# Two decode layers on one core: one batch's first block of K kept in a PSUM bank between the layers, and one bank for all small and idle products

## The chip, the cores and the metric

The kernel runs on one core of a Trainium2 chip, in one launch. The metric is the device time of a launch in microseconds (us). Every engine of the core (TensorE or PE, VectorE or DVE, ScalarE or ACT, GpSimd or POOL, SyncE or SP) has its own queue of instructions; the queues meet through semaphores, which the tile framework sets from the regions that instructions read and write.

## The reference

A decode step for 4 batch rows of width 512: an attention block and a gated feed-forward, and then both again with the same weights and the same K and V caches. All values are fp32. Cut to what matters:

```python
B, D, Hq, Hkv, Sk, Dh, F = 4, 512, 32, 8, 4096, 128, 1792
def A(x):                                    # attention against the cache
    q = heads(x @ wq)                        # 32 heads; 4 of them share one of 8 K/V groups
    p = softmax(q . k_cache * Dh ** -0.5)    # 4096 keys
    return concat(p @ v_cache) @ wo
def Bf(x):                                   # gated feed-forward
    return (silu(x @ w1) * (x @ w3)) @ w2
x = x + A(layernorm(x)); x = x + Bf(layernorm(x))
x = x + A(layernorm(x)); x = x + Bf(layernorm(x))
```

K and V hold 4 x 8 x 4096 x 128 values each, 64 MB a cache and 128 MB for both, and each layer needs all of them. On chip there is room for some 27 MB, so almost everything is read twice.

## The kernel before, in words

**Storage.** One SBUF tile, `arena`, holds everything that is loaded: 216 units of 256 fp32 columns (`KB`), 128 KB of data to a unit over the 128 partitions. `take` and `give` hand out units when the program is built, `load` appends an entry to a list `plan`, and `pump` issues the next entries of that list on SyncE's DMA queue (L183) as soon as their units are free in the list's bookkeeping; on the chip each issue then waits until the engines have done with what lay there. So the order of loads is fixed by hand, and each load goes out when its place falls free. `loaded` names the units of a key, `done` and `vacate` free them.

**Attention.** The groups of K/V heads are worked in turn, 0 to 7 in the first layer and 7 to 0 in the second, so that group 7 (`TURN`) ends one layer and begins the next; its V, and `wq` and `wo`, stay in the arena. `scores` multiplies the padded queries `qpad` with K in 8 blocks (`NB`) of 512 keys (`BK`); in each block it has one matmul for each batch row `b` (L393), all into the bank `s_ps`. `factors` and `exponents` make the softmax's numerators, `turn_p` transposes them, `weigh` multiplies them with V into `o_ps` (L438), and `project_o` adds `oT` times `wo` to `x_ps`, either by `whole` (two matmuls of 512 columns, L473) or by `pair` (four of 256, L466).

**The turn between the layers.** In the first layer's feed-forward (`feed_forward`, `keep` true) w1, w3 and w2 pass through 7 slots of 4 units that are used round and round. Behind the last piece of w2 the same slots take K of group 7 for its first 4 blocks (`SPLIT`) in pieces called `half`: 8 pieces, 2 to a block, each for 2 of the 4 batch rows. Piece 7 and what follows go where `wq` lies, and so wait for the second layer's Q products (`q_product`, L337). `collect` closes a residual sum: it copies `x_ps` to the SBUF tile `p` (L314, L316), turns it by matmuls into a small product in PSUM (L320, L323), adds that to `xc` (L324), and returns `mean`, a further small product (L329) that VectorE subtracts from `mu` (L330). `project_q` then makes the queries: it copies the first group's Q product to `p`, turns it (`q_turn`, L348) into `qpad` (L374), and yields the products of the other groups as steps that stand between other work on PE.

**Small and idle products.** `misc` hands out a small PSUM area, from the two banks `m_ps0` and `m_ps1` in turn. `busy(n)` puts matmuls on PE whose result nobody reads (L281), up to three units of 128 columns in each, into the bank that `misc` did not hand out last. The sum of squares of a layer norm is such a small product too (`total`, L290, read at L300).

PSUM has eight banks: `s_ps`, `o_ps`, `t_ps`, `x_ps`, `m_ps0`, `m_ps1`, and `kept0` and `kept1`, in which `stash` keeps the first piece of `wo` over the turn.

Of the kernel before, what the change touches and what calls it, by code (L numbers as in the profile page):

```python
# [8 lines left out]
F32 = mybir.dt.float32  # L9
# [7 lines left out]
P = 128  # L17
KC = D // P
NB = 8
BK = SK // NB  # L20
# [12 lines left out]
TURN = HKV - 1  # L33
# [5 lines left out]
def tile_decode_layers(ctx: ExitStack, tc: tile.TileContext, x, kt, v, wq, wo, w1, w3, w2, w2s, out):  # L39
    nc = tc.nc  # L40
# [3 lines left out]
    psum = ctx.enter_context(tc.tile_pool(name="psum", bufs=1, space=bass.MemoryType.PSUM))  # L44
# [72 lines left out]
    def piece(name, i, at):  # L117

        w, layer, lo, n, per = {"w1a": (w1, 0, 4 * i, 4, 4), "w3a": (w3, 0, 4 * i, 4, 4),
                                "w1b": (w1, 0, 16 + 3 * i, 3, 3), "w3b": (w3, 0, 16 + 3 * i, 3, 3),  # L120
                                "w2": (w2, 0, 4 * i, 4, 2), "half": (kt[TURN], 1, 4 * i, 4, 4)}[name]
        weights(name, w[:, lo * KB:(lo + n) * KB], layer, (n,), per, at, 2 * i if name == "w2" else i)

    RING = KEPT + 64
# [67 lines left out]
    def loaded(*key):  # L192
        a, n, _ = where[key]
        return arena[:, a * KB:(a + n) * KB]
# [60 lines left out]
    o_ps = psum.tile([P, 512], F32, name="o_ps")  # L255
    t_ps = psum.tile([P, 4, P], F32, name="t_ps")
    x_ps = psum.tile([P, 512], F32, name="x_ps")
    m_ps = [psum.tile([P, 512], F32, name=f"m_ps{i}") for i in range(2)]
    kept = [psum.tile([P, 512], F32, name=f"kept{i}") for i in range(2)]
    nc.vector.memset(x_ps, 0.0)  # L260

# [6 lines left out]
    turn = {"m": 0}  # L268

    def misc(n=B):  # L270
        turn["m"] ^= 1
        return m_ps[turn["m"]][:, 0:KC * n].rearrange("p (k c) -> p k c", k=KC)

    def flat(a):
        return a.rearrange("p k b -> p (k b)")
# [1 line left out]
    def busy(n=1):  # L277

        while n > 0:
            w = min(n, 3)  # L280
            nc.tensor.matmul(m_ps[turn["m"] ^ 1][0:32, (4 - w) * P:], rows, ident.unsqueeze(1).broadcast_to([P, w, P]),  # L281
                             start=True, stop=True)
            n -= w

# [66 lines left out]
    def project_q(layer, steps, mean):  # L351
        one_ps = t_ps.rearrange("p i r -> p (i r)")
        sq = squares()
        q_product(layer, steps[0], one_ps, 0, True, True)
        m = total(flat(sq))
        q_copy(one_ps)
        rstd = deviation(sq, m)
        nc.vector.tensor_scalar(scaled, rows, rstd, SCALE, op0=ALU.mult, op1=ALU.mult)
        rest = list(enumerate(steps[1:]))

        def products():
            for j, g in rest:
                q_product(layer, g, o_ps, j, j == 0, j == HKV - 2)
                yield
            q_copy(o_ps)
            yield
            nc.vector.tensor_copy(qT, q_turn(32))
            yield
        more = products()
        if layer:  # L370
            next(more)
            next(more)
        m = q_turn(B)
        nc.vector.tensor_copy(qpad[:, :, PAD:PAD + REP], m.rearrange("p h b -> p b h"))  # L374
        if layer:
            next(more)
        mean()
        return more
# [5 lines left out]
    def scores(layer, g, pieces=iter(())):  # L384
        for blk in range(NB):
            split = layer == 1 and g == TURN and blk < SPLIT
            keys = [("half", layer, 2 * blk + i) for i in range(2)] if split else [("k", layer, g, blk)]
            lo = PAD - REP * blk
            for i, key in enumerate(keys):
                k = loaded(*key).rearrange("p (b s) -> p b s", s=BK)  # L390
                for j in range(B // len(keys)):
                    b = i * B // len(keys) + j
                    nc.tensor.matmul(s_ps[32 * b:32 * b + 32, :], qpad[:, b, lo:lo + 32], k[:, j, :],  # L393
                                     start=(blk == 0), stop=(blk == NB - 1))
            for key in keys:
                done(*key)
            next(pieces, None)
# [32 lines left out]
    def weigh(layer, g, st, pieces=iter(()), fill=False):  # L430
        for f in range(2):
            for i in range(NI):
                if fill and f and i == NI // 2:
                    busy(9)
                key = ("v", 0 if g == TURN else layer, g, NI * f + i)
                w = loaded(*key).rearrange("p (b n) -> p b n", b=B)
                for b in range(B):
                    nc.tensor.matmul(o_ps[32 * b:32 * b + 32, :], pT[:, i, 32 * b:32 * b + 32], w[:, b, :],  # L438
                                     start=(i == 0), stop=(i == NI - 1))
                if g != TURN or layer:  # L440
                    done(*key)
                yield
            next(pieces, None)
            if f == 0:
                nc.scalar.activation(p, o_ps, AF.Copy, scale=st["parts"][:, 0:1])  # L445
            else:
                nc.vector.scalar_tensor_tensor(p, o_ps, st["parts"][:, 1:2], p, op0=ALU.mult, op1=ALU.add)  # L447
        if fill:
            busy(2)
        for j in range(4):  # L450
            nc.tensor.transpose(t_ps[:, j, :], p[:, j * P:(j + 1) * P], ident)  # L451
        if fill:
            busy()

        own = t_ps[:, :, :]
        own = bass.AP(own.tensor, own.offset, [own.ap[0], (1, REP), (32, B), (P + 4, 4), (16, 2)])
        raw = small("raw", REP * B)
        nc.vector.tensor_reduce(raw.rearrange("p (h b) -> p h b", b=B), own, axis=AX.XY, op=ALU.add)
        nc.vector.tensor_tensor(oT[:, g].rearrange("p h b -> p (h b)"), raw, st["r"], op=ALU.mult)  # L459
# [24 lines left out]
    def project_o(layer, g, first=False, last=False):  # L484
        for i in range(2):
            n = 2 * g + i
            key = ("wo", 0, n)
            w = loaded(*key).rearrange("p (h e) -> p h e", e=D)
            if last or not layer and g == TURN - 1:
                pair(i, lambda h: oT[:, g, h, :], lambda j: w[:, j, :], False, last and i == 1)  # L490
            else:
                whole(i, lambda h: oT[:, g, h, :], lambda j: w[:, j, :], first)
            if layer or n == 0:
                vacate(*key)
            if not layer and i == (g < TURN):
                busy({3: 6, 5: 3, 6: 2, 7: 2}.get(g, 0))

    def feed_forward(layer, mean):
        keep = layer < LAYERS - 1
# [48 lines left out]
        if not keep:  # L548
            for k in range(KC):
                nc.tensor.matmul(x_ps[32 * k:32 * k + B, 0:P], xt[:, k, :], ident, start=True, stop=False)  # L550
            busy(5)
        gate(0, FA)
        join(0, FA)
        product("w1b", s_ps, FA, FB, (1, 1, 1, 1))
# [48 lines left out]
    for layer in range(LAYERS):  # L603
# [28 lines left out]
        if layer == 0:  # L632
            give(PT, ARENA - PT)
            pump()
            stash()

            busy(15)
            for g in range(HKV):
                project_o(layer, g, g == 0, g == TURN)
        else:  # L640
            project_o(layer, before[0], False, True)
# [46 lines left out]
```

## Time and profile before

| | before |
|---|---|
| time, median of 3 runs | 705.85 us (705.85 to 705.91) |
| the profiled execution | 705.91 us |
| its span, first to last instruction | 704.1 us |
| read from HBM | 298.85 MB, 425 GB/s over the span |
| PE, VectorE, ScalarE busy | 408.4, 85.1, 36.8 us (58, 12 and 5%) |
| mean granted clock of PE | 0.81 of full speed |

How to read it: busy shares are means over stages. The share of busy DMA engines and the GB/s in a window say whether the stream of loads runs without a gap. The chain of waits is followed back from the last instruction and says what the end hung on. In a row of the timeline the first number is the start, the second the duration, and what stands in brackets is how long the engine was idle before it and what released it. An fp32 matmul is two passes over PE, so it counts twice in "x".

### The profile page before, as it was taken

How to read it: one execution, taken by the hardware profiler on the slowest of the kernel's cores; microseconds unless marked ns; L12 is line 12 of the kernel's file. 1: busy time of each engine (PE TensorE's matmuls, PEld its weight loads, DVE VectorE, ACT ScalarE, POOL GpSimd, SP SyncE). 2: the span in 40 equal slices, each digit the busy share in tenths (PEclk: the TensorE clock that was granted, in tenths of full speed). 3: DMA queues.
4: the chain of work that ended last, by engine and by line, in shares of the span. 5: the costliest groups of instructions: out<-in, count | busy, mean ns of one | idle time of the engine just before them, and what ended most of it. 6: DMA issues, size and time to landing. Idle time of an engine off the chain costs nothing. (4 is left out here: it accounts for less than half of the span.)

```text
span 704.1 us, 7082 instructions
## 1 busy us (share of the span) xinstructions
PE 408.4 (58%) x3174; PEld 136.0 (19%) x3174; DVE 85.1 (12%) x291; ACT 36.8 (5%) x85; POOL 2.9 (0%) x10
## 2 busy tenths in 40 slices
PE   2555453456556454547788894364553545477687
PEld 1112011112111111112243231021120111122134
DVE  2001010101001010101111111011000101010111
ACT  0000000000000000002001000000000000000100
POOL 0000000000000000000000000000000000000000
PEclk9986787767777776879999988679787868689899
DMA  9999999999999999999999999999999999999997
GB/s 417 432 403 473 418 417 422 462 418 432 451 421 422 436 448 421 440 408 435 410 405 403 410 437 440 439 436 422 432 455 417 433 432 440 421 433 420 426 425 298
DMA packets 13749, 299.37 MB, mean 425 GB/s; under 512 B 1671, under 2 KB 1799, under 8 KB 6407
## 3 DMA queue, kind: packets, MB, share of 16 engines
q1 hardware_dynamic: 13584, 298.92, 99.2%
q8 instruction: 25, 0.41, 0.2%
q14 instruction: 5, 0.04, 0.0%
q10 hardware_dynamic: 135, 0.01, 0.0%
HBM read 298.85 MB, written 0.07 MB: 425 GB/s over the span
## 5 line engine op out<-in xcount | busy, mean ns | idle before, releaser
L438 PE MATMUL o_ps<-arena 128*32 128x512 f32 x1024 | 148.6, 730 | 147.8 <-DMA arena<-in_v 133.0
L393 PE MATMUL s_ps<-arena,qpad 128*32 128x512 f32 x1024 | 146.2, 725 | 88.0 <-DMA arena<-in_kt 88.0
L438 PEld LDWEIGHTS o_ps<-arena 128*32 128x32 f32 x1024 | 37.7, 130 | 256.8 <-issue 224.5
L393 PEld LDWEIGHTS s_ps<-arena,qpad 128*32 128x32 f32 x1024 | 39.3, 130 | 178.1 <-issue 170.6
L447 DVE SCALAR_TENSOR_TENSOR p<-o_ps,parts,p 128x512 f32<-128x512 f32 x16 | 12.0, 751 | 272.7 <-PE o_ps L438 272.7
L400 DVE TENSOR_REDUCE top<-s_ps 128x1 f32<-128x512 f32 x16 | 11.1, 691 | 190.8 <-PE s_ps L393 190.8
L281 PE MATMUL m_ps<-ident,rows 128*32 128x256 f32 (+2 forms) x90 | 25.2, 376 | 0.0
L445 ACT ACTIVATE p<-o_ps,parts 128x512 f32<-128x512 f32 x16 | 11.0, 687 | 195.8 <-PE o_ps L438 186.9
L337 PE MATMUL o_ps<-arena,xpad 128*32 128x512 f32 x112 | 15.4, 675 | 7.8 <-DMA arena<-in_wq 7.8
L424 PE MATMUL t_ps<-ident,p 128*128 128x128 f32 x64 | 11.4, 305 | 13.5 <-ACT p L418 13.5
L451 PE MATMUL t_ps<-ident,p 128*128 128x128 f32 x64 | 10.5, 287 | 13.9 <-DVE p L447 13.8
L411 ACT ACTIVATE f<-d 128x1 f32<-128x1 f32 x16 | 3.2, 203 | 253.1 <-DVE d L409 253.1
L473 PE MATMUL x_ps<-arena,oT 128*4 128x512 f32 x104 | 12.8, 592 | 6.3 <-DVE oT L459 3.5
L418 ACT ACTIVATE p<-s_ps,top 128x512 f32<-128x512 f32 x16 | 10.9, 684 | 76.7 <-PE t_ps L451 76.7
L425 DVE COPY arena<-t_ps 128x512 f32<-128x512 f32 x16 | 11.1, 691 | 9.7 <-PE t_ps L424 9.7
L451 PEld LDWEIGHTS t_ps<-ident,p 128*128 128x128 f32 x64 | 6.7, 141 | 28.0 <-DVE p L447 28.0
L424 PEld LDWEIGHTS t_ps<-ident,p 128*128 128x128 f32 x64 | 7.3, 150 | 22.3 <-ACT p L418 19.2
L281 PEld LDWEIGHTS m_ps<-ident,rows 128*32 128x32 f32 x90 | 9.4, 110 | 10.4 <-issue 6.3
L506 PE MATMUL o_ps<-arena,xpad 128*32 128x192 f32 (+1 forms) x128 | 8.1, 360 | 1.3 <-DMA arena<-in_w 1.2
L506 PE MATMUL s_ps<-arena,xpad 128*32 128x192 f32 (+1 forms) x128 | 7.9, 359 | 1.6 <-DMA arena<-in_w 1.5
L337 PEld LDWEIGHTS o_ps<-arena,xpad 128*32 128x32 f32 x112 | 3.6, 122 | 17.2 <-DMA arena<-in_wq 8.7
L533 PE MATMUL x_ps<-arena,qT 128*4 128x128 f32 (+1 forms) x168 | 5.9, 271 | 1.1 <-DMA arena<-in_w 1.1
(100 smaller groups left out, 137.3 us busy)
## 6 DMA issues: line engine op xcount, KB each, us to landing
arena<-in_v SPq DMA_DIRECT2D x4, 4096.0 KB, 37.3
arena<-in_w SPq DMA_DIRECT2D x17, 512.0 KB, 9.3
arena<-in_kt SPq DMA_DIRECT2D x8, 1024.0 KB, 10.5
arena<-in_kt SPq DMA_DIRECT2D x2, 4096.0 KB, 16.9
arena<-in_wq SPq DMA_DIRECT2D x1, 7168.0 KB
arena<-in_v SPq DMA_DIRECT2D x3, 2048.0 KB, 36.9
arena<-in_wo SPq DMA_DIRECT2D x1, 4096.0 KB, 24.5
arena<-in_kt SPq DMA_DIRECT2D x8, 512.0 KB, 8.0
```

The costliest lines, as they stand in the source:

```text
L281: nc.tensor.matmul(m_ps[turn["m"] ^ 1][0:32, (4 - w) * P:], rows, ident.unsqueeze(1).broadcast_to([P, w, P]), start=True, stop=True)
L337: nc.tensor.matmul(ps[32 * k:32 * k + 32, :], xpad[:, k, lo:lo + 32], w[:, k, :], start=first, stop=last)
L393: nc.tensor.matmul(s_ps[32 * b:32 * b + 32, :], qpad[:, b, lo:lo + 32], k[:, j, :], start=(blk == 0), stop=(blk == NB - 1))
L400: nc.vector.tensor_reduce(top[:, 0:1], s_ps, axis=AX.X, op=ALU.max, negate=True)
L424: nc.tensor.transpose(t_ps[:, i, :], p[:, i * P:(i + 1) * P], ident)
L425: nc.vector.tensor_copy(pT.rearrange("p i r -> p (i r)"), t_ps.rearrange("p i r -> p (i r)"))
L438: nc.tensor.matmul(o_ps[32 * b:32 * b + 32, :], pT[:, i, 32 * b:32 * b + 32], w[:, b, :], start=(i == 0), stop=(i == NI - 1))
L445: nc.scalar.activation(p, o_ps, AF.Copy, scale=st["parts"][:, 0:1])
L447: nc.vector.scalar_tensor_tensor(p, o_ps, st["parts"][:, 1:2], p, op0=ALU.mult, op1=ALU.add)
L451: nc.tensor.transpose(t_ps[:, j, :], p[:, j * P:(j + 1) * P], ident)
L473: nc.tensor.matmul(x_ps[r:r + B, :], left(2 * i + n), w(n), start=first, stop=False)
L506: nc.tensor.matmul(ps[32 * j:32 * j + 32, lo:lo + n], x32[:, k, :], w[:, j * n:(j + 1) * n], start=(k == 0), stop=(k == KC - 1))
```

## The change

In the first layer, once PE has issued the matmuls of group 7's block 0, ScalarE copies batch row 0's 512 columns of that block to a PSUM bank of their own, `keptk`. In the second layer, after the turned query has been copied out, ScalarE copies them back to `p`, and the score matmul of row 0 and block 0 reads `p`. Piece 0 of `half` is then 2 units (row 1 alone) in place of 4, so 256 KB less are loaded. The bank comes from `m_ps`: `misc` hands out columns 0 to 127 and 128 to 255 of one bank in turn, and `busy` writes columns 256 to 511 of the same bank, at most two units a matmul. Some counts of `busy` are smaller, and group 6's projection in the first layer goes by `whole`.

```diff
-                                "w2": (w2, 0, 4 * i, 4, 2), "half": (kt[TURN], 1, 4 * i, 4, 4)}[name]
+                                "w2": (w2, 0, 4 * i, 4, 2), "half": (kt[TURN], 1, 4 * i if i else 2, 4 if i else 2, 4 if i else 2)}[name]
...
-    m_ps = [psum.tile([P, 512], F32, name=f"m_ps{i}") for i in range(2)]
+    m_ps = psum.tile([P, 512], F32, name="m_ps")
+    keptk = psum.tile([P, BK], F32, name="keptk")
...
         turn["m"] ^= 1
-        return m_ps[turn["m"]][:, 0:KC * n].rearrange("p (k c) -> p k c", k=KC)
+        lo = P * turn["m"]
+        return m_ps[:, lo:lo + KC * n].rearrange("p (k c) -> p k c", k=KC)
...
-            w = min(n, 3)
-            nc.tensor.matmul(m_ps[turn["m"] ^ 1][0:32, (4 - w) * P:], rows, ident.unsqueeze(1).broadcast_to([P, w, P]),
+            w = min(n, 2)
+            nc.tensor.matmul(m_ps[0:32, (4 - w) * P:], rows, ident.unsqueeze(1).broadcast_to([P, w, P]),
...
         if layer:
+            nc.scalar.copy(p, keptk)
             next(more)
...
-                    nc.tensor.matmul(s_ps[32 * b:32 * b + 32, :], qpad[:, b, lo:lo + 32], k[:, j, :],
+                    if split and b < 2 and blk == 0:
+                        this = k[:, 0, :] if b else p
+                    else:
+                        this = k[:, j, :]
+                    nc.tensor.matmul(s_ps[32 * b:32 * b + 32, :], qpad[:, b, lo:lo + 32], this,
...
+            if g == TURN and blk == 0 and not layer:
+                nc.scalar.copy(keptk, loaded(*keys[0])[:, 0:BK])
...
@@ weigh
-                    busy(9)
+                    busy(6)
...
@@ project_o
-            if last or not layer and g == TURN - 1:
+            if last:
...
-                busy({3: 6, 5: 3, 6: 2, 7: 2}.get(g, 0))
+                busy({3: 6, 5: 2, 6: 2, 7: 2}.get(g, 0))
...
@@ feed_forward
-            busy(5)
+            busy(4)
...
@@ tile_decode_layers
-            busy(15)
+            busy(14)
```

## The prediction, made before the changed kernel was run

> **What bounds the kernel now.** I read the head of the page first, then the end of the chain of waits, then windows and the timeline around the turn between the layers, and last the timeline of the tail.
>
> ```profile
> DMA  9999999999999999999999999999999999999997
> HBM read 298.85 MB, written 0.07 MB: 425 GB/s over the span
> ```
> All 40 slices but the last show the 16 DMA engines nine tenths busy or more: the span is the time of 298.85 MB.
>
> ```profile
> 685.54 15.05 DMA arena<-in_w
> 700.63 0.45 PE x_ps L533 x8
> ```
> This is how the chain of waits ends: the last weights are issued at 685.54 and land 15.05 us later behind everything queued before them; from 700.63 PE, VectorE and the output's transfer take the remaining 3.5 us of the span of 704.1. The end is therefore set by bytes, unless the queue runs empty somewhere or PE falls behind the stream in the tail.
>
> ```profile
> 363.00:373.00 10.00, 8.10 (x101) 3.61 (x93) 1.18 (x4) 1.91 (x3) 0.00 (x0) 1.00 1.03 404
> 375.00:388.00 13.00, 11.30 (x106) 4.58 (x104) 2.44 (x12) 0.85 (x3) 0.55 (x1) 1.00 1.02 401
> ...
> 386.00:388.00 2.00, 2.00 (x19) 0.54 (x19) 0.89 (x5) 0.37 (x1) 0.55 (x1) 1.00 1.03 412
> 388.00:390.00 2.00, 2.00 (x21) 1.14 (x17) 0.17 (x1) 0.00 (x0) 0.00 (x0) 1.00 1.07 385
> 390.00:392.00 2.00, 2.00 (x22) 0.82 (x22) 0.16 (x1) 0.00 (x0) 0.00 (x0) 1.00 0.97 379
> 392.00:394.00 2.00, 2.00 (x24) 0.65 (x20) 0.00 (x0) 0.00 (x0) 0.00 (x0) 1.00 1.02 401
> ```
> These windows end in granted clock, DMA share and GB/s. The first holds mostly pieces of 384 KB (3 KB a partition), the second pieces of 512 KB (4 KB a partition): 404 against 401 GB/s, so row length hardly matters there. The four slices are the place to watch: at 388 to 392 the rate falls to 385 and 379 between 412 and 401. Against 412 that is 27 and 33 GB/s for 2 us each, 0.12 MB or 0.3 us. Here the queue is lean.
>
> **The change, part by part.**
>
> *Fewer bytes.* Piece 0 of the half shrinks from 512 to 256 KB: batch 0 of block 0 is no longer read again. At the stage's 401 GB/s, 262,144 bytes are 0.65 us; at the span's 425 they are 0.62; at the slowest slice of the turn, 379, they are 0.69. What remains has rows of 2 KB, which no run shows by themselves. At worst such a row takes as long as one of 4 KB, and the saving is 0; the nearest rows, 3 KB at 404, say that time follows bytes. I take 0.65.
>
> *The copy into the kept bank (layer 0).*
>
> ```profile
> 299.44 4.48 PE L393 MATMUL s_ps<-arena,qpad 128*32 128x512 f32 x40
> 300.55 3.76 SPq L183 DMA_DIRECT2D arena<-in_v  x4
> 305.73 0.20 ACT L411 ACTIVATE f<-d 128x1 f32<-128x1 f32 x1 [16.59 <-DVE d L409]
> ```
> ```profile
> L418 ACT ACTIVATE p<-s_ps,top 128x512 f32<-128x512 f32 x16 | 10.9, 684 | 76.7 <-PE t_ps L451 76.7
> ```
> The added ScalarE copy of 128x512 costs about 0.68 us (the L418 group). It waits for group 7's K, as PE does at 299.44, so it runs to about 300.2. ACT has been idle for 16.59 us before 305.73, so nothing is queued behind it. The buffer's next user is the DMA of 300.55, later than the copy's end. Cost 0; without that cover the load would be issued up to 0.7 us later, and with nothing else queued the stream would be late by as much.
>
> *The copy back (layer 1).*
>
> ```profile
> 388.00 1.05 PE L348 MATMUL m_ps<-scaled,p 128*128 128x4 f32 x8
> 389.09 0.17 DVE L374 COPY qpad<-m_ps 128x16 f32<-128x16 f32 x1 [1.41 <-PE m_ps L348]
> 389.98 0.38 PE L329 MATMUL m_ps<-off,both 128*128 128x4 f32 x2
> 390.29 1.06 PE L393 MATMUL s_ps<-arena,qpad 128*32 128x512 f32 x8
> 402.13 1.06 PE L393 MATMUL s_ps<-arena,qpad 128*32 128x512 f32 x8 [1.05 <-DMA arena<-in_kt]
> ```
> ACT may overwrite `p` when PE has read it, at 389.05, and ends near 389.8; the first score matmul comes at 390.29. There is 0.5 us of cover from the third Q product. Without it PE would lose at most the 0.7, and it waits 1.05 us for K at 402.13 anyway. ACT has no other work before the second half of Q is copied, after all Q products. Cost 0. SP and GpSimd are passed by neither copy, and the number of DMAs stays.
>
> *One bank for small products and idle products.* Column ranges stay apart, but the bank is now shared, so a write of PE must wait until VectorE has read the last small product.
>
> ```profile
> 383.19 0.38 ACT L316 ACTIVATE p<-x_ps 128x256 f32<-128x256 f32 x1 [11.44 <-DVE p L314]
> 384.18 0.37 PE L323 MATMUL m_ps<-off,both 128*128 128x16 f32 x2
> 384.49 0.41 PE L281 MATMUL m_ps<-ident,rows 128*32 128x128 f32 x2
> 384.60 0.17 DVE L324 TENSOR_TENSOR xpad<-xpad,m_ps 128x16 f32<-128x16 f32 x1 [0.74 <-PE m_ps L323]
> 384.82 1.06 PE L337 MATMUL t_ps<-arena,xpad 128*32 128x512 f32 x8
> ```
> That disjoint halves of one bank are kept apart is seen already: ScalarE takes columns 256 to 511 of `x_ps` only when VectorE has done with columns 0 to 255 (its row at 383.19 was released by VectorE's L314, which reads those). [...] By address alone the next two costs would be 0 and the sum unchanged, since both are covered.
>
> First, the idle product that ends `collect`. It now runs under VectorE's add (384.49 beside 384.60). With one bank it starts only after that read, at 384.8, exactly when the next real product could, and pushes it by its own length: 0.21 us if passes follow each other (9 units take 2.10 us below, with 0.2 of fill), 0.41 if not. Three places; I take 0.21 each.
>
> ```profile
> 684.74 0.36 PE L329 MATMUL m_ps<-off,both 128*128 128x4 f32 x2
> 684.93 0.17 DVE L300 SCALAR_TENSOR_TENSOR sq<-m_ps,pick 128x16 f32<-128x16 f32 x1 [2.14 <-PE m_ps L290]
> 685.10 1.93 PE L506 MATMUL o_ps<-arena,xpad 128*32 128x256 f32 x32
> ...
> 688.88 1.51 PE L506 MATMUL s_ps<-arena,xpad 128*32 128x192 f32 x32 [0.57 <-DMA arena<-in_w]
> 697.45 1.06 PE L533 MATMUL x_ps<-arena,qT 128*4 128x128 f32 x32 [0.45 <-DMA arena<-in_w]
> ```
> Second, `mean` in each feed-forward: L329 follows the sum of squares, which VectorE reads at 684.93 to 685.10. It slides from 684.74 to about 685.1, and the products behind it, with VectorE's update of the mean, by 0.36. Elsewhere the reader is long done before PE returns to the bank (389.26 against 389.98).
>
> Do these delays reach the end? In the tail PE waits 0.57 and 0.45 us for weights. It is late by 0.21 + 0.36, and `busy(5)` to `busy(4)` gives back 0.21: net 0.36, which is less than the 0.57 at 688.88. Everything before that starts from V's landing and moves up with the stream. Cost 0; were that wait under 0.36, the rest would pass into the end.
>
> *Fewer idle products, and `whole` for `pair`.*
>
> ```profile
> 672.62 2.10 PE L281 MATMUL m_ps<-ident,rows 128*32 128x384 f32 x6
> 675.29 1.92 PE L438 MATMUL o_ps<-arena 128*32 128x512 f32 x16 [0.58 <-DMA arena<-in_v]
> ...
> 352.39 1.05 PE L466 MATMUL x_ps<-arena,oT 128*4 128x256 f32 x16
> 424.05 1.04 PE L473 MATMUL x_ps<-arena,oT 128*4 128x512 f32 x8
> ```
> `busy(9)` to `busy(6)` takes 3 x 0.21 us from a stretch after which PE waits 0.58 for V: 0, and it lets PE take V up to 0.65 earlier. Group 6's projection by `pair` takes 1.05 us in 16 matmuls, `whole` 1.04 in 8: 0.
>
> *The lean queue at the turn.*
>
> ```profile
> 382.72 0.33 SPq L183 DMA_DIRECT2D arena<-in_kt  x1
> 385.92 0.33 SPq L183 DMA_DIRECT2D arena<-in_kt  x1
> ```
> ```profile
> arena<-in_kt SPq DMA_DIRECT2D x8, 512.0 KB, 8.0
> out<-p SPq DMA_DIRECT2D x1, 64.0 KB, 1.6
> ```
> After 382.72 the next load waits for the first Q product and is issued 3.2 us later. A 512 KB piece lands 8.0 us after its issue, of which about 1.6 is latency (what the lone output transfer takes) and 1.3 its own move: some 5.1 us are queued ahead as a rule. Pieces come 1.3 us apart while the stream is even, so the gap uses up 1.9 and leaves 3.2, or 1.6 beyond the latency, as an estimate and a mean over 16 engines. The change takes 0.65 of queued work and adds 0.21 of delay: 0.7 us left. Since the rate dips already, some engines run dry sooner. The loss lies between 0 (the last engine never runs dry) and 0.86 (it has no margin now). I take 0: 0.7 stays positive, and what counts at the end is the engine that finishes last.
>
> **Sum.** -0.65 + 0 = -0.65. The profiled execution took 705.91, the median is 705.85: 705.26 against the first, 705.20 against the second. I predict 705.2, 0.09% faster. About 0.2%, 1.41 us, is what a measurement of this kernel can tell from no change.
>
> **Rivals.**
> *Nothing gained* (0.18): the turn eats it, or rows of 2 KB move at half the rate: 705.85; with the whole 0.86 lost, 706.06. For it: 385 and 379 GB/s at 388 to 392. Against: the 0.7 us left.
> *More than the bytes* (0.10): the dip of 0.3 us closes too, as the copy leaves less to fetch before the turn: 704.9. Against: Q's product, not the piece, sets the issue at 385.92.
> *Slower, by the clock* (0.06).
>
> ```profile
> 404.00:406.00 2.00, 0.12 (x1) 0.13 (x2) 1.18 (x6) 0.87 (x3) 0.00 (x0) 0.62 1.03 430
> ```
> ```profile
> 338.81 3.41 PE L281 MATMUL m_ps<-ident,rows 128*32 128x384 f32 x10
> 344.98 3.62 PE L473 MATMUL x_ps<-arena,oT 128*4 128x512 f32 x32 [2.75 <-DMA arena<-in_wo]
> ```
> PE idles 2.75 us before 344.98, and `busy(14)` makes that 2.96. If the granted clock halves there, as it does at 404 (0.62 in the first row) after a gap of 2.7 (403.19, the end of the score matmuls that began at 402.13, to 405.88), the 3.62 us of projection become 7.2 and the loads that wait for them go out up to 3.6 late. With no cover from the queue that gives 708.8. It decides for "slower" when over 2.06 of it (the 0.65 gained and 1.41) passes the cover; against it stands a cover of some 5 us as long as pieces follow each other evenly. [...]
>
> **Chances and range.** The forecast has 0.64, and 0.02 is left for what no row shows. Faster by over 1.41 us has 0.05: 0.04 of the 0.10, should more than the dip close, and half of the 0.02, since no row has 1.41 us to give. Slower by over that has 0.07: the clock case and the other half. The rest lies within 1.41 us: 0.88. The range runs from the closed dip, with 0.1 beyond it, to the turn that loses all 0.86, with 0.1 beyond it: 704.8 to 706.2.
>
> **What the profile after would show.** HBM read 298.59 MB; an ACT copy of 0.7 us at 299.5 and one near 389; the last idle product of `collect` behind VectorE's add, and L329 behind L300; the last weights landing 0.65 earlier; at 388 to 392 a rate not under 375. Wrong would be: a slice at the turn far below that, PE no longer waiting for weights at 688 and 697, or a clock under 1.00 between 340 and 400.

## The result, and the profile after

| | before | after |
|---|---|---|
| time, median of 13 runs each, run beside each other | 706.01 us (705.85 to 706.93) | 707.82 us (706.34 to 708.88) |
| ratio, with its 95% interval | | 1.002 (1.0013 to 1.0028) |
| the profiled execution, its span | 705.91, 704.1 us | 707.88, 706.1 us |

By the medians the changed kernel is 1.8 us slower (0.9 to 2.0 by the interval), where 0.65 us less were forecast. Fewer bytes were read, as told, and the rate fell by more. The page of the changed kernel:

```profile
HBM read 298.59 MB, written 0.07 MB: 423 GB/s over the span
```
298.59 MB is the figure of the prediction. Three long windows tell where the rate was lost. Each row ends in granted clock, DMA share and GB/s; first the kernel before, then the changed one.

```profile
340.00:376.00 36.00, 29.59 (x289) 11.68 (x288) 4.53 (x16) 2.86 (x6) 0.55 (x1) 1.00 1.01 406
376.00:400.00 24.00, 22.84 (x209) 9.27 (x201) 2.79 (x14) 1.22 (x4) 0.55 (x1) 1.00 1.01 402
400.00:690.00 290.00, 170.88 (x1261) 53.97 (x1264) 37.26 (x118) 15.56 (x37) 0.55 (x1) 0.81 1.00 431
```
```profile
340.00:376.00 36.00, 29.09 (x286) 12.15 (x285) 4.62 (x16) 2.85 (x6) 0.56 (x1) 1.00 1.01 406
376.00:400.00 24.00, 22.68 (x197) 8.78 (x193) 2.88 (x14) 1.75 (x5) 0.55 (x1) 0.93 0.98 384
400.00:690.00 290.00, 170.02 (x1248) 53.31 (x1240) 37.36 (x118) 15.62 (x38) 0.55 (x1) 0.82 1.00 431
```
Ahead of the turn and behind it the rates are the same. In the 24 us of the turn 18 GB/s are missing: 0.43 MB, or 1.07 us at 402 GB/s. That is more than the 0.65 us that the smaller piece saves. The slices of 2 us (the columns as before) show where:

```profile
384.00:386.00 2.00, 1.74 (x14) 0.95 (x14) 0.35 (x2) 0.00 (x0) 0.00 (x0) 0.71 1.04 414
386.00:388.00 2.00, 2.00 (x11) 0.71 (x10) 0.73 (x4) 0.29 (x1) 0.00 (x0) 0.50 0.76 305
388.00:390.00 2.00, 2.00 (x19) 0.52 (x11) 0.27 (x2) 0.08 (x1) 0.55 (x1) 0.94 0.93 297
390.00:392.00 2.00, 2.00 (x17) 1.14 (x17) 0.17 (x1) 0.59 (x1) 0.00 (x0) 1.00 0.88 293
392.00:394.00 2.00, 2.00 (x21) 0.68 (x24) 0.16 (x1) 0.00 (x0) 0.00 (x0) 1.00 1.03 418
```
Before, these slices had 412, 385, 379 and 401 GB/s from 386 on, at a clock of 1.00. Now they have 305, 297 and 293, and the clock is at 0.50 from 386 to 388. The timeline of PE, SyncE's queue and ScalarE there (start, duration; in brackets the idle time and its releaser):

```profile
384.76 0.40 PE L283 MATMUL m_ps<-ident,rows 128*32 128x128 f32 x1 [0.26 <-DVE xpad L326]
384.78 1.08 PE L339 MATMUL t_ps<-arena,xpad 128*32 128x512 f32 x3
384.95 0.42 PE L283 MATMUL m_ps<-ident,rows 128*32 128x128 f32 x1
385.17 1.91 PE L339 MATMUL t_ps<-arena,xpad 128*32 128x512 f32 x5
```
```profile
387.13 0.33 SPq L183 DMA_DIRECT2D arena<-in_kt  x1
```
```profile
390.87 0.59 ACT L378 COPY p<-keptk 128x512 f32<-128x512 f32 x1 [2.79 <-PE m_ps L350]
```
The idle product (L283) waits for VectorE's add, as told. The first Q product (L339), which took 1.06 us before, stretches from 384.78 to 387.08 at the halved clock, so the load behind it goes out at 387.13 in place of 385.92. The copy back takes 0.59 us and is done before the scores' first matmul with `p` at 392.01.

The end of the chain of waits:

```profile
686.30 15.67 DMA arena<-in_w
702.01 0.62 PE x_ps L542 x16
702.67 0.45 PE x_ps L542 x8
```
The last weights land near 702.6, where before they did at 700.6. The turn accounts for less than half of that. The trace has a completion record for each of the 16 DMA engines of a load; these are the records of the last load of weights. The column beside them is a sum over all packets of the trace: how much of the stream was still to come at 690, in us at 420 GB/s, as a difference to the kernel before.

```
          still to come at 690   median engine   last but one   last engine
before           0                  700.3           700.6          700.6
after          +0.46                700.2           701.8          702.6
```
The median engine is done 0.1 us earlier than before, the last one 2.0 later. So two things are to be explained: the loss at the turn, and a last engine that falls behind.

### The profile page after: what moved, and what is told of

The parts are those of the page before. It is cut to its first block, busy times and chain, and to the rows that moved or that the text cites. A ratio compares the mean times of both kernels' runs of the same rounds, so it can differ in the third digit from the quotient of the medians.

```text
span 706.1 us, 7079 instructions
## 1 busy us (share of the span) xinstructions
PE 409.9 (58%) x3172; PEld 136.9 (19%) x3172; DVE 85.4 (12%) x291; ACT 38.0 (5%) x87; POOL 2.9 (0%) x10
## 3 DMA queue, kind: packets, MB, share of 16 engines
HBM read 298.59 MB, written 0.07 MB: 423 GB/s over the span
## 5 line engine op out<-in xcount | busy, mean ns | idle before, releaser
L447 PE MATMUL o_ps<-arena 128*32 128x512 f32 x1024 | 146.8, 722 | 145.7 <-DMA arena<-in_v 130.7
L400 PE MATMUL s_ps<-arena,qpad 128*32 128x512 f32 x1022 | 149.3, 738 | 88.9 <-DMA arena<-in_kt 88.7
L283 PE MATMUL m_ps<-ident,rows 128*32 128x256 f32 (+1 forms) x96 | 24.1, 352 | 0.8 <-DVE xpad L326 0.8
L339 PE MATMUL o_ps<-arena,xpad 128*32 128x512 f32 x112 | 16.1, 702 | 7.4 <-DMA arena<-in_wq 7.4
L283 PEld LDWEIGHTS m_ps<-ident,rows 128*32 128x32 f32 x96 | 10.1, 110 | 10.8 <-issue 3.5
L339 PEld LDWEIGHTS o_ps<-arena,xpad 128*32 128x32 f32 x112 | 3.7, 126 | 17.4 <-issue 9.0
```

The lines of the kernel that those rows point to most:

```text
L283: nc.tensor.matmul(m_ps[0:32, (4 - w) * P:], rows, ident.unsqueeze(1).broadcast_to([P, w, P]), start=True, stop=True)
L339: nc.tensor.matmul(ps[32 * k:32 * k + 32, :], xpad[:, k, lo:lo + 32], w[:, k, :], start=first, stop=last)
```

## The experiments

In the table stand all kernels, ordered by what lies at the turn (e1 to e13 are the experiments below): the rate from 376 to 400, what was still to come at 690, and the landing of the last weights (median and last engine) are of each kernel's one profiled execution; the last two columns are of all its runs. The kernel before stood at 706.01 to 706.4 us beside them.

```
                                GB/s      to come  median, last     profiled  median    ratio to before
                                376-400   at 690   engine           us        us        (95%)
piece 0 whole
  before                        402        0       700.3   700.6    705.91    706.01    -
  one bank only (e1)            398       +0.64    700.8   701.2    706.65    706.50    1.0002 (0.9993-1.0011)
  no last idle product (e4)     408       +0.13    700.8   701.0    706.36    706.78    1.0003 (0.9994-1.0012)
  two VectorE more (e5)         405       +0.40    701.0   701.9    707.18    706.85    1.0006 (0.9998-1.0015)
  two transfers (e11)           407       -0.16    700.5   701.4    706.58    706.50    1.0005 (0.9997-1.0014)
  load 0.45 later (e9)          406       -0.19    700.2   701.8    710.22    706.31    1.0008 (0.9999-1.0016)
  load 1.23 later (e10)         386       +0.85    700.6   702.8    708.24    708.29    1.0025 (1.0015-1.0035)
piece 0 short
  after                         384       +0.46    700.2   702.6    707.88    707.82    1.002  (1.0013-1.0028)
  two banks (e2)                395       +0.37    700.5   702.7    708.49    707.75    1.0014 (1.0005-1.0022)
  idle product elsewhere (e3)   399       -0.33    699.8   702.3    707.52    707.52    1.0013 (1.0004-1.0022)
  stash on ScalarE (e6)         392       +0.18    700.2   702.3    707.83    707.93    1.0023 (1.0011-1.0035)
  e2 with that stash (e8)       396       -0.19    699.9   701.3    706.91    706.88    1.0011 (1.0000-1.0021)
  e2, busy tail (e13)           393       +0.07    700.1   702.9    708.31    707.83    1.0022 (1.0013-1.0032)
fewer bytes, cover kept
  later piece (e7)              413       -0.88    699.8   700.1    705.37    706.12    0.9995 (0.9987-1.0003)
  short piece, cover back (e12) 407       -0.28    700.1   701.1    706.27    706.36    1.0007 (0.9998-1.0016)
```

**The shared bank alone (e1).** Only the bank is shared, and nothing is kept.

```diff
-    m_ps = [psum.tile([P, 512], F32, name=f"m_ps{i}") for i in range(2)]
+    m_ps = psum.tile([P, 512], F32, name="m_ps")
...
-        return m_ps[turn["m"]][:, 0:KC * n].rearrange("p (k c) -> p k c", k=KC)
+        lo = P * turn["m"]
+        return m_ps[:, lo:lo + KC * n].rearrange("p (k c) -> p k c", k=KC)
...
-            w = min(n, 3)
-            nc.tensor.matmul(m_ps[turn["m"] ^ 1][0:32, (4 - w) * P:], rows, ident.unsqueeze(1).broadcast_to([P, w, P]),
+            w = min(n, 2)
+            nc.tensor.matmul(m_ps[0:32, (4 - w) * P:], rows, ident.unsqueeze(1).broadcast_to([P, w, P]),
```


> The kernel before with one bank for small and idle products (offsets and two units a matmul as in the change); nothing kept, bytes as before. Clock theory (the idle product that ends collect now runs behind VectorE's add, PE's window at the turn holds less work, the granted clock halves there, and the lean queue of loads runs dry): the first Q product of the second layer takes about 2 us in place of 1.1 in profiles where the clock falls, GB/s at 386 to 392 under 350, time 0.5 to 2 us above before. Cover theory (the queue runs dry because the shortened piece leaves 0.65 us less queued): no change, 705.9 to 706.2. Bank-wait theory (only the waits themselves, 0.2 to 0.4 us each, without the clock): at most 0.4 above before, clock 1.00 throughout the turn.

706.50 us, ratio 1.0002: the waits that the bank adds cost nothing that can be told, as the prediction had it.

**The smaller piece alone (e2).** Two banks as before, the piece short; in place of a kept copy `p` is written from `t_ps`, so this kernel, and e8 and e13 after it, leaves the scores of row 0 and block 0 out of its result. The score matmul reads `p` as in the change.

```diff
-                                "w2": (w2, 0, 4 * i, 4, 2), "half": (kt[TURN], 1, 4 * i, 4, 4)}[name]
+                                "w2": (w2, 0, 4 * i, 4, 2), "half": (kt[TURN], 1, 4 * i if i else 2, 4 if i else 2, 4 if i else 2)}[name]
...
         if layer:
+            nc.scalar.copy(p, one_ps)
             next(more)
```


> The kernel before with the shortened first piece and the score matmul of batch row 0, block 0 reading p; two banks and the idle products as before. No bank is left for K, so p is filled by a ScalarE copy of the same size out of t_ps: the scores of that row and block are left out of the computation, and the copy in the first layer is not made. Clock theory: the clock stays at 1.00 through the turn, and the 0.65 us of bytes come through, 705.2 to 705.5. Cover theory: the turn runs dry without any help from the clock, 705.9 to 707. Bank-wait theory: as the clock theory, 705.2 to 705.5.

707.75 us: the part that was to bring the gain brings the loss. Its profiled execution has a full clock at the turn, and the dip is there all the same (clock, DMA share and GB/s at the end of each row):

```profile
386.00:388.00 2.00, 2.00 (x22) 0.71 (x18) 0.67 (x4) 0.37 (x1) 0.55 (x1) 1.00 1.02 401
388.00:390.00 2.00, 2.00 (x20) 1.12 (x16) 0.42 (x2) 0.29 (x1) 0.00 (x0) 1.00 0.91 356
390.00:392.00 2.00, 2.00 (x22) 0.71 (x18) 0.16 (x1) 0.30 (x1) 0.00 (x0) 1.00 0.92 346
392.00:394.00 2.00, 2.00 (x24) 0.63 (x20) 0.00 (x0) 0.00 (x0) 0.00 (x0) 1.00 0.98 373
```
356, 346 and 373 GB/s stand against 385, 379 and 401 before.

**The idle product that waits for the add (e3, e4).** In e3 the changed kernel's last idle product of `collect` goes to `t_ps`, so that it does not wait; in e4 the kernel before does without it.

```diff
-        busy()
+        busy(1, t_ps.rearrange("p i r -> p (i r)"))
```


> The changed kernel with the one idle product that ends collect written to t_ps, which nobody reads then, so that it runs under VectorE's add again. Clock theory: first Q product 1.1 us, clock 1.00 at the turn, 705.2 to 705.8. Cover theory: still dry at the turn, 706.5 to 708. Bank-wait theory: 0.2 us better than the changed kernel's 707.8 and no more.

> The kernel before without the idle product that ends collect; banks and bytes as before. Clock theory: with that work gone the clock falls at the turn in some executions, and the time is 0.5 to 2 us above before. Cover theory and bank-wait theory: nothing waits longer and no byte is moved, so no change, 705.9 to 706.2.

e3 took 707.52, e4 706.78 with 1.0003. In e3's profiled execution the clock is at 1.00 across the turn, the load goes out at 385.79 as before, and the rate sinks nevertheless:

```profile
386.00:388.00 2.00, 2.00 (x18) 0.55 (x18) 0.76 (x5) 0.37 (x1) 0.55 (x1) 1.00 1.03 391
388.00:390.00 2.00, 2.00 (x18) 1.14 (x18) 0.17 (x1) 0.59 (x1) 0.00 (x0) 1.00 0.92 360
390.00:392.00 2.00, 2.00 (x22) 0.79 (x26) 0.16 (x1) 0.00 (x0) 0.00 (x0) 1.00 1.04 383
392.00:394.00 2.00, 2.00 (x24) 0.56 (x20) 0.00 (x0) 0.00 (x0) 0.00 (x0) 1.00 0.95 365
```
So neither the idle product's place nor the halved clock of the one execution is needed for the slower median. In the one execution in which the clock fell there, the dip was the deepest: 384 GB/s over the turn, against 392 to 399 in the five others with a short piece.

**Instruction fetches (e5, e6, e8).** The page lists 25 packets of instructions of 16 KB and 5 of 8 KB, and counts them as a share of the same 16 DMA engines. VectorE's list of instructions is two longer in the changed kernel (324 records in its trace in place of 322, two of them semaphore waits), and by the records of those packets a fetch of 8 KB that came at 702.5 us before comes at 696.8, amid the last loads. e5 adds two small memsets to VectorE's list in the kernel before; e6 takes the two copies of `stash` off VectorE in the changed kernel, e8 in e2.

```diff
-            nc.vector.tensor_copy(kept[i], loaded("wo", 0, 0)[:, i * D:(i + 1) * D])
+            nc.scalar.copy(kept[i], loaded("wo", 0, 0)[:, i * D:(i + 1) * D])
```


> The kernel before with two more VectorE instructions, one-column memsets of a tile that nobody reads, in the second layer (at restore); bytes, banks and idle products as before. Fetch theory (the change makes VectorE's queue two instructions longer, by two waits; so the next 8 KB block of its instructions is fetched at 696 in place of 702.5, ahead of the last weights on one of the 16 DMA engines, and that engine lands last): an 8 KB instruction packet near 696, the last engine of the last load 1 us or more behind the others, time 0.5 to 1.5 us above before. Cover theory (the turn runs dry because less is queued there): no change from before. Clock theory: no change.

> The changed kernel with the two copies of stash on ScalarE in place of VectorE: VectorE's queue is three instructions shorter than in the change and one shorter than before. Fetch theory: the 8 KB packet goes back to 702, after the last weights, and the time comes down by 0.8 to 1.5 us from the changed kernel's 707.8, to 706.2 to 707. Cover theory: unchanged, 707.3 to 708. Both at work: about 706.5, as the turn still eats the 0.65 of bytes.

> The second experiment (fewer bytes, two banks, p filled out of t_ps, so that the scores of row 0 and block 0 are left out) with the copies of stash on ScalarE. Fetch theory: 1 us below that experiment's 707.75, 706.0 to 706.8. Cover theory: unchanged, 707.5 to 708. Its difference to e6 is what the shared bank costs: under 0.4 us by the bank-wait theory, up to 1 by the clock theory.

e5's fetch came at 696.3, and the kernel took 706.85 (1.0006, not to be told from 1; its interval leaves room for up to 1 us). In e6 the fetch went back to 706.5, and the kernel took 707.93 with its last engine at 702.3 behind a median of 700.2. So the loss is there without the fetch at 696. e8, whose interval of 1.0000 to 1.0021 reaches into both groups, decides nothing.

The completion records leave the fetch a share all the same. In the changed kernel, e2, e3, e11, e12 and e13 it comes at 695.6 to 696.8, and there the last engine's lag behind the median grows by 0.6 to 0.95 us from the load whose median engine lands near 694 to the one near 697. In the eight kernels where it comes behind 702 the lag grows by 0.03 us at most. But e5 has the fetch without the growth, so the link is not proven. In the changed kernel it is 0.85 of a lag of 2.4 us; 1.9 were there before it, where the kernel before had 0.4.

**The same bytes off a later load (e7).** e6, but with batch row 0 of block 7 kept: the pieces at the turn are whole, and the 256 KB are taken off the last load of group 7's K, when more is queued: in the kernel before that load (1 MB) goes out at 392.28 and lands 8.7 us later by the mean of the engines, the load behind the wait (512 KB) 4.7 us after its issue.

```diff
-    cache("k", 1, TURN, (8,) * (NB - SPLIT), SPLIT)
+    cache("k", 1, TURN, (8,) * (NB - 1 - SPLIT), SPLIT)
+    load(kt[TURN][:, (8 * (NB - 1) + 2) * KB:8 * NB * KB], 6, [("k", 1, TURN, NB - 1)])
```


> As e6, but what is kept is batch row 0 of block 7 in place of block 0, copied back to p after the second Q copy; the pieces of half are whole again and the 256 KB come off the last load of group 7's K, where the queue is full. Fetch theory with the cover theory: no straggler and no loss at the turn, so the 0.65 come through: 705.0 to 705.9, 0.3 to 0.9 below the kernel before beside it. Fetch theory alone: the same as e6. Cover theory alone: 706.3 to 707.5.

```profile
386.00:388.00 2.00, 2.00 (x19) 0.68 (x18) 0.91 (x5) 0.37 (x1) 0.55 (x1) 1.00 1.02 408
388.00:390.00 2.00, 2.00 (x20) 1.12 (x16) 0.17 (x1) 0.00 (x0) 0.00 (x0) 1.00 1.05 416
390.00:392.00 2.00, 2.00 (x22) 0.84 (x22) 0.16 (x1) 0.00 (x0) 0.00 (x0) 1.00 1.03 414
```
No dip, and 0.88 us less to come at 690, the 0.65 among them. 706.12 us is 1.8 below e6, which differs from it only in which row is kept: where the bytes come off and when they are copied back. Against the kernel before (706.33 beside it) the ratio of 0.9995 has 1 in its interval: a gain of 0.2 us is not shown.

**A later load, whole pieces (e9, e10).** In the kernel before, three or six units of idle product ahead of the second layer's first Q product.

```diff
         sq = squares()
+        if layer:
+            busy(3)
         q_product(layer, steps[0], one_ps, 0, True, True)
```


> The kernel before, with its pieces and bytes as they are; only three units of idle product (0.64 us by the nine that take 2.10) stand on PE ahead of the second layer's first Q product, so the load that waits for this product is issued some 0.64 us later, near 386.5. Theory (too little is queued at the turn): this takes about as much cover as the 256 KB did; the windows from 388 to 392 fall to some 300 to 350 GB/s and the time rises by 0.5 to 1.5 us over the kernel before's, though no piece is short and no byte is saved. First rival (the short piece itself, its rows of 2 KB or the order it gives the engines, costs the time): no short piece here, so within 0.3 us of the kernel before. Second rival (the prediction's own reckoning, 0.7 us of cover left at such a delay): no change either.

> As the run before, with six idle units (1.28 us by the same rate), so that the load goes out near 387.2. Theory (too little is queued at the turn): past the point where the queue is used up, each further 0.64 us of delay is lost in full: 0.5 to 0.8 us above the run with three units, 1.1 to 2.3 above the kernel before. First rival (the short piece): as the kernel before, within 0.3 us. Second rival (0.7 us of cover left): 0.4 to 0.8 above the kernel before, and the run with three units at 0.

The load behind the wait in SyncE's queue, first e9 and then e10, and e10's slices:

```profile
386.37 2.52 SPq L183 DMA_DIRECT2D arena<-in_kt  x3
```
```profile
387.15 1.66 SPq L183 DMA_DIRECT2D arena<-in_kt  x2
```
```profile
386.00:388.00 2.00, 2.00 (x19) 0.69 (x15) 0.67 (x4) 0.27 (x1) 0.00 (x0) 1.00 0.95 379
388.00:390.00 2.00, 2.00 (x19) 0.92 (x12) 0.24 (x1) 0.10 (x1) 0.55 (x1) 1.00 0.96 317
390.00:392.00 2.00, 2.00 (x21) 0.83 (x24) 0.33 (x2) 0.00 (x0) 0.00 (x0) 1.00 0.89 313
```
With the load at 387.15, 1.23 us late, the kernel before shows what the changed kernel showed: 317 and 313 GB/s, 386 over the turn, +2.2 us, a last engine at 702.8. No byte and no bank was touched. e9 is a miss of the theory's number: idle products fit partly between the Q product's matmuls (one starts at 384.98, between L337's at 384.75 and 385.20), so the load was only 0.45 us late (386.37); the turn kept 406 GB/s, and the median rose 0.2 us (1.0008, with 1 in the interval), not 0.5 to 1.5. So some cover is there, more than 0.45 us and less than 1.23. Three of e9's runs took 708.6 to 710.2. The profiled one, 710.22, has a clock of 0.50 from 694 to 704, and in it 6.6 us pass from the last landing to the end of the span, where the kernel before needs 3.5.

**Two short transfers (e11).** The kernel before, with piece 0 as two transfers of 256 KB.

```diff
-            nc.sync.dma_start(arena[:, a * KB:(a + n) * KB], src)
             i = state["next"]
+            two = len(keys) == 1 and keys[0] == ("half", 1, 0)
+            for lo, hi in ((0, n // 2), (n // 2, n)) if two else ((0, n),):
+                nc.sync.dma_start(arena[:, (a + lo) * KB:(a + hi) * KB], src[:, lo * KB:hi * KB])
```


> The kernel before, with the first half piece loaded by two transfers of 256 KB (2 KB a partition each) in place of one of 512 KB; the bytes and all else stay. Theory (too little is queued at the turn): as many bytes are queued, so within 0.3 us of the kernel before and 380 to 400 GB/s from 388 to 392. Rival (rows of 2 KB, or a transfer so short, cost time or set the 16 engines apart): 0.5 to 1.5 us slower, the more so as there are two of them, with one engine that ends 0.7 us or more behind the others.

407 GB/s over the turn and 706.50: rows of 2 KB cost nothing that can be told.

**The cover given back (e12).** The changed kernel; half of piece 7 goes into the two units that the short piece 0 leaves free, and so is issued ahead of the wait.

```diff
     for i in range(7):
         piece("half", i, slots[i])
+    piece("half", 7, slots[0] + 2)
     ring["to"] = len(plan) - 1
-    piece("half", 7, None)
+    piece("half", 8, None)
```
The scores of block 3 read the three parts where they lie.

> The changed kernel, with piece 7 of the half as two transfers of 256 KB: batch row 2 of block 3 goes into the two units that the short piece 0 leaves free and is issued before the wait for the second layer's first Q product; row 3 follows where piece 7 did. As many bytes as before the change are then queued at that wait, and the 256 KB fewer are taken off behind it. Theory (too little is queued at the turn): the loss at the turn falls to that of the kernel before, and the time comes to 705.2 to 706.2 us, 1.3 to 2 us below the changed kernel; should the dip only move behind the smaller transfer, 706.2 to 707. Rival (it is the shared bank, the fewer idle products, short pieces or the instruction fetches): it stays at 707 to 708.

```profile
376.00:400.00 24.00, 22.49 (x204) 8.89 (x205) 2.79 (x14) 1.80 (x5) 0.55 (x1) 1.00 1.02 407
```
407 GB/s where the changed kernel had 384, and 706.36 us where it had 707.82; bank, copies, counts of idle products and the total of bytes are the changed kernel's. That is most of the loss, though not a gain over the kernel before (1.0007, with 1 in the interval; 705.72 to 709.0).

**The clock in the tail (e13).** e2's profiled execution shows a halved clock in the tail too, behind waits of 1.03 and 0.45 us for weights:

```profile
694.00:696.00 2.00, 2.00 (x40) 1.09 (x35) 0.19 (x1) 0.00 (x0) 0.00 (x0) 0.63 1.02 422
696.00:698.00 2.00, 2.00 (x35) 1.01 (x26) 0.22 (x1) 0.00 (x0) 0.00 (x0) 0.50 0.90 353
698.00:700.00 2.00, 2.00 (x39) 1.39 (x43) 0.18 (x1) 0.00 (x0) 0.00 (x0) 0.50 0.73 287
```
e13 is e2 with those waits filled: `busy(5)` to `busy(9)`, and a `busy(2)` ahead of the last product with w3.

> The kernel before with fewer bytes (the short piece, two banks) and more idle products in the tail: four units more (0.85 us) ahead of the product that waited 1.03 us for weights, two more (0.42) ahead of the one that waited 0.45. Theory A (the clock, halved in the tail after those waits, makes part of the lost time): no halved slice from 692 to 702, and 706.2 to 707.0 against the 707.75 without them. Theory B (the last of the 16 engines sets the end, whatever the clock): 707.3 to 708.2, as without them. Rival (PE becomes the bound there): slower still, by up to 1.3.

In its execution the clock stayed at 1.00 up to the last matmul, and the median was 707.83 as without the filling. This is the end of its chain:

```profile
702.33 0.62 PE x_ps L538 x16
...
702.98 0.45 PE x_ps L538 x8
```
PE waits for a load whose last engine lands at 702.9. The clock in the tail lengthens single executions (with the profiled one of e9 6.6 us after the last landing, not 3.5); the slower median stands without it.

## Why the prediction was wrong

*Right:* 298.59 MB; the idle product behind the add (PE idle for 0.26 us ahead of 384.76, released by VectorE's L326); `mean` behind the sum of squares (0.28 us ahead of 686.13, released by VectorE's L302); the shared bank at no measurable cost (e1). Fewer idle products and `whole` were not tried alone; e7, which has them, is not slower than the kernel before. The copies cost nothing visible; the first one runs at 294.92 for 0.59 us, with block 0's matmuls, not near 299.5 as I had written. In the changed kernel's execution the fall of the clock near 345 did not come (PE waits 2.81 us there, and the clock stays at 1.00). It came at the turn, where nothing in the profile of before had shown it. In e3, e7 and e12, which have the change's idle products, it did come near 345. This is the projection in the changed kernel, and then in e7 with the clock behind it:

```profile
344.91 3.62 PE L482 MATMUL x_ps<-arena,oT 128*4 128x512 f32 x32 [2.81 <-DMA arena<-in_wo]
```
```profile
344.91 5.31 PE L484 MATMUL x_ps<-arena,oT 128*4 128x512 f32 x32 [2.25 <-DMA arena<-in_wo]
346.00:348.00 2.00, 2.00 (x12) 0.34 (x8) 0.00 (x0) 0.05 (x1) 0.00 (x0) 0.50 0.97 410
```

*Wrong:* the step "The lean queue at the turn", taken as 0 out of 0 to 0.86. It measured, from 376 to 400, 1.07 us in the changed kernel (with the halved clock) and, from the same rows of the others, (402 - 399) x 24 / 402 = 0.2 us in e3 to 0.6 in e6 (392 GB/s) at full clock. The kernels with whole pieces, e10 apart, had 398 to 408, so against a typical 406 it is some 0.4 to 0.8: the saving of 0.65 is gone in the 24 us in which it was to be made. e12 and e7 keep the queue as full as before and get the rate back; e10 takes the cover away by a delay alone and has the loss. That too little queued at the wait costs the rate at the turn is shown by these three.

The reckoning went astray in two places. The first is the 1.6 us of cover "beyond the latency", a mean over the 16 engines. They did not run abreast. The completion records of the last piece that is queued ahead of the wait, engine by engine, set against the issue of the next load:

```
            issue     first engine    median   last    engines done within 1.6 us of the issue
before      385.92       387.9        389.2    390.9           0 of 16
e9          386.37       387.9        388.9    390.8           4
after       387.13       387.4        388.2    390.3          12
e10         387.15       388.0        388.9    390.9           8
```
The first engine in the kernel before is through 2.0 us after the issue, the median 3.3, the last 5.0. With 1.6 of latency (the lone output transfer) the cover begins at 0.4 us, not 1.6, and the lead of the first engines is spent waiting. e9, late by 0.45, lies at that edge; the changed kernel has 12 engines dry. With 1.6 the count is still kind: those 12 engines stood idle and landed the next piece 3.1 to 3.4 us after its issue, and less the 1.3 of its own move that leaves 1.8 to 2.1 us of latency, an estimate, where the lone transfer gave 1.6. No run here shows what the latency is made of.

The second place is that only one wait was counted. The two loads behind it, of 1 MB each, wait for further Q products (in the kernel before they go out at 387.27 and 388.13), and the queue is no fuller for them. This is what each of the three loads lost: the step from the mean landing (over the 16 engines) of the load ahead of it to its own, less what that step is in the even stream (1.27 us for 512 KB, 2.49 for 1 MB, 0.65 for the 256 KB of e12).

```
            behind the wait   next    third   sum, us
before           0.05         0.33    0.14    0.52
e9               0.33         0.11    0.10    0.54
e10              0.58         0.73    0.24    1.55
after            0.95         0.75    0.11    1.81
e2               0.06         0.64    0.25    0.95
e3               0.03         0.55    0.30    0.88
e6               0.17         0.65    0.34    1.16
e12              0.02         0.34    0.10    0.46
e7               0.00         0.06    0.09    0.15
```
e2 and e3, whose first engine is done 1.6 and 1.7 us after the issue, lose next to nothing at the load behind the wait, as the count has it, and 0.64 and 0.55 us at the next one, where the kernel before loses 0.33. e9 loses at the first load what it then does not lose at the second, so its delay costs nothing. The sums are of one execution each: e1, with whole pieces, has 0.90, and its median is not told from that of the kernel before.

The other wrong step was the sentence beside it, that the end goes by the engine that finishes last. The end does go by that engine, but this was taken as a reason for no loss, and that engine came later. In e13, e3, e6 and the changed kernel the median engine ends 0.1 to 0.5 us earlier than before and the last 1.7 to 2.3 us later; in e7 and e12 the last is 0.5 earlier and 0.5 later. It explains most of the difference in those executions: e3 had 0.33 us less to come at 690 than the kernel before, and its last weights landed 1.7 later. Which engine it is and why it falls behind stays open: the records give no packet's engine. That leading engines, having lost their lead at the turn, no longer absorb the instruction fetches behind it is only argued; the fetch at 696 may be a part of it, and e6 has the late engine without that fetch. e5, e9 and e11 have a last engine 0.9 to 1.5 behind the median with whole pieces, so a short piece is not needed for it, and each number here is of one execution.

*The rivals.* "Nothing gained", at 0.18, had the right place (the turn eats it) and, with 706.06 at most, too small a price: it counted the 0.86 as an even loss and no engine that ends late. "Slower by the clock" had a halved clock as mechanism, at 345. It came there in e3, e7 and e12 and cost far less than the 3.6 us: the clock was back after 3.4 us (a mean of 0.95 from 340 to 376 in each of the three), the projection took 1.7 us longer (5.31 against 3.62), and the load behind it went out at 349.8, as in the changed kernel; e7 has the lowest median of the experiments. The fall at 404 in the kernel before, which this rival leant on, came some 1.3 us into the gap that begins at 403.19 (clock 1.00 from 404.0 to 404.4, 0.50 from 404.6), not behind the whole 2.7; yet at 345 the clock was still at 1.00 after 2.75 us without work. At the turn one execution had a halved clock at 384.8, and the slower median stands without it (e2, e6 and e13 had it at neither place).

## What to carry to other kernels

Where a load waits for an engine, count the cover by the DMA engine that is done first, not by the mean: in this stream the 16 engines were 3 us apart, and a mean of 3.3 us after the issue hid a first of 2.0. Count it for every load until the queue is deep again; in e2 and e3 the loss lay at the second. Bytes saved ahead of such a wait are also bytes that covered it; take them off where the queue is deep (e7: 413 GB/s over the turn, against 392 in e6 for the same bytes), or put other loads in their place ahead of the wait (e12). Where the end moves by more than the stream does, as here, read the landing of the last load engine by engine.

## What the runs showed of the hardware that I had not expected

- The 16 DMA engines drift apart: 387.9 to 390.9 us for one piece of 512 KB (DMA share 1.01 from 376 to 400), and 696.8 to 700.6 for the last load in the kernel before.
- A halved clock behind short waits, where a wait of 2.81 us at 345 had left it whole. At that place it fell in e3, e7 and e12 behind waits of 2.14 to 2.30 us. In e2, e3 and e9 it fell between 692 and 696 behind waits of 0.45 to 1.2 us, and in e6 it did not behind waits of 1.40 and 0.45. In the changed kernel it fell at 384.8 and was at 0.50 up to 388.2; these are the 3.4 us ahead of the fall and the 3.4 behind it, first in the kernel before, then in the changed one (PE's busy time is the second number, the clock the third from the end):

```profile
381.40:384.80 3.40, 3.04 (x25) 1.72 (x22) 0.76 (x4) 0.47 (x2) 0.00 (x0) 1.00 1.02 404
384.80:388.20 3.40, 3.40 (x29) 1.07 (x28) 1.08 (x6) 0.37 (x1) 0.55 (x1) 1.00 1.02 411
```
```profile
381.40:384.80 3.40, 2.76 (x26) 1.62 (x25) 0.82 (x5) 0.47 (x2) 0.00 (x0) 1.00 1.02 404
384.80:388.20 3.40, 3.40 (x16) 1.22 (x20) 0.88 (x5) 0.37 (x1) 0.00 (x1) 0.50 0.89 340
```
PE was busy 2.76 of 3.40 us ahead of the fall, against 3.04 where there was none. What sets it off is not settled here.
- A delay of 0.45 us for one load cost nothing that can be told (e9); one of 1.23 us cost 2.2 us at the median (e10; 1.1 to 2.5 by the interval).
